# Transposing u by DMA on the SyncE queue in place of TensorE matmuls, in a retention-and-mixer kernel

## The chip, the cores and the metric

The kernel runs on one core of one Trainium2 chip. The metric is the time on the device in microseconds (us), the median of several runs. A core has five engines that run side by side and wait for each other by semaphores: TensorE (PE, matrix products into PSUM), VectorE (DVE), ScalarE (ACT), GpSimd (POOL) and SyncE (SP, which here only issues DMAs). DMAs move data by 16 DMA engines that all queues share. Each engine and each queue takes its instructions strictly in its own order: an instruction that waits holds up all behind it on that engine.

## The reference

Four batches of 768 tokens, 8 heads of 64, so a model width of 512. First a retention layer gives x, then a mixer:

```python
# retention, for each head h with decay gamma[h]
state = gamma * state + k[t] (outer) v[t]
y[t]  = scale * q[t] @ state
x     = y, heads side by side             # (4, 768, 512)
# mixer
h  = x^T @ U @ V                          # along the tokens, rank 32
u  = x + h^T
ch = relu(u @ w_ch1) @ w_ch2              # 512 -> 2048 -> 512
out = u + ch
```

## The kernel before

The retention is computed in chunks of 128 tokens, six chunks to a batch, in bf16 with sums in fp32. The program is software-pipelined over the batches. Batch 0's retention runs first (turn0, score0, mix0, L484 to L536), while the first weights are loaded. After that there are four stages. In stage b the MLP of batch b-1 is computed on PE in 64 groups of matmuls ("pieces", mlp_pieces), and woven in between them is the retention of batch b (turn_chunk, score4, mix4) and the low-rank part of the mixer. The last stage has the MLP of batch 3 alone.

One MLP runs in this order on PE: 16 groups "up" (L414) over tokens 0 to 511, each of four 128x512 matmuls, then 16 groups "up" over tokens 512 to 767, each of four 128x256 matmuls, then 24 groups "down" (L437) of four. ACT (L421) and DVE (L419) take the up results through the ReLU into gT, DVE adds u to the down results (L442), and POOL's queue stores them (L403).

The "up" matmuls need u with the model width on the partitions: uT[b], of 4 blocks of 128 by 768 tokens. u itself is made with the tokens on the partitions. Three functions make u and uT:

- lr_proj(b) (L366) projects x of the whole batch by U, so it needs all six chunks.
- lr_expand(b, j0, nj) (L375) multiplies by V for nj groups of 128 tokens, and DVE adds x and writes u (L382).
- lr_turn(b, j0) (L387) turns two groups of 128 tokens: eight matmuls against the identity (L391) into the PSUM tile R, and one copy by ACT into uT (L395, recorded as L75, the line of the helper evac).

For batch 0, tokens 0 to 511 are turned and summed in another way (x_turn, and L577 to L581); only its tokens 512 to 767 go by lr_turn. For batches 1 to 3, lr_turn is called three times: for tokens 0 to 255 and 256 to 511 towards the end of the stage in which the batch's retention is computed, and for 512 to 767 early in the stage in which its MLP runs.

The order on each engine is the order in which the program text issues it (manual_schedule). weave goes through the pieces of an MLP, and before each piece calls the marks whose place, a share of the MLP's nominal cost, has been reached. The places of lr_turn are these:

```python
LR = {1: (0.89, 0.92, 0.945, 0.97), 2: (0.71, 0.75, 0.83, 0.89)}   # proj, expand, turn, turn
marks = [(0.02, part(lr_expand, b - 1, 4, 2)), (0.06, part(lr_turn, b - 1, 4))]   # b > 1
marks = [(0.03, part(lr_expand, 0, 4, 2)), (0.10, part(lr_turn, 0, 4)), ...]      # b == 1
```

Loads of q, k, v and the weights are all issued by SP, in the order of the list feed. The function feed_more issues as many of them as there are free buffers, whenever a buffer is given up in program order (19 buffers in the pool rin; one buffer each for qin and kin, in which batches 1 to 3 hold all of q or k, loaded by load_whole, L115; the others are loaded at L142). POOL casts and scales the loaded chunks to bf16 (prep_turned, prep_natural, L86 and L88). A batch's kin and qin are loaded only once POOL has cast the last chunk of the batch before. In program order these loads are issued well ahead of the marks of lr_turn: when lr_turn(0, 4) is called, all loads of batch 1 have been put into SP's queue, and when the first lr_turn of batch b is called, all those of batch b+1.

The uT and u tiles have two buffers each, so that the batches take turns.

Of the kernel before, what the change touches and what calls it, by code (L numbers as in the profile page):

```python
# [16 lines left out]
def kernel(  # L17
# [11 lines left out]
    nc = tc.nc  # L29
    P = 128  # L30
# [6 lines left out]
    NCB = DM // P  # L37
# [22 lines left out]
    R = [psum.tile([P, 2, 512], fp32, tag="r0", name="r0")]  # L60
# [12 lines left out]
    def evac(eng, dst, src):  # L73
        if eng == "A":
            nc.scalar.activation(dst, src, AF.Copy)  # L75
        else:
            nc.vector.tensor_copy(out=dst, in_=src)
# [106 lines left out]
    for h in range(H):  # L184
        r = ds(32 * (h // 2), 32)
# [6 lines left out]
    ident = consts.tile([P, P], bf16)  # L192
# [4 lines left out]
    for i in range(NST):  # L197
        t = consts.tile([P, 4, P], bf16, name=f"state{i}")
# [157 lines left out]
    us, uTs, pcs = {}, {}, {}  # L356
# [27 lines left out]
                R[g][:, :, :nj * P].rearrange("p c (j e) -> p c j e", j=nj),  # L384
                v4(xs[b][:, ds(j0, nj), e]), op=ALU.add)

    def lr_turn(b, j0, eng="A"):  # L387
        r = R[j0 // 2 % 2]
        for c in range(NCB):
            for jj in range(2):  # L390
                nc.tensor.matmul(r[:, c // 2, ds(256 * (c % 2) + P * jj, P)],  # L391
                                 us[b][:, j0 + jj, ts(c, P)], ident, start=True,
                                 stop=True)
        evac(eng, uTs[b][:, :, ds(j0 * P, 2 * P)],
             r.rearrange("p n (c t) -> p (n c) t", c=2))  # L395


    stores = []

# [147 lines left out]
    with tc.tile_pool(name="psum0", bufs=1, space=bass.MemoryType.PSUM) as psum0:  # L547
# [21 lines left out]
        for j in range(NCK):  # L569
            for c in range(NCB):  # L570
                nc.tensor.matmul(p_p[ds(RK * c, RK), :P], Ub[:, j],
                                 xs[0][:, j, ts(c, P)], start=(j == 0),
                                 stop=(j == NCK - 1))
# [27 lines left out]
    for b in range(1, B):  # L601
        w = min(b, 2)
        if b > 1:
            marks = [(0.02, part(lr_expand, b - 1, 4, 2)),
                     (0.06, part(lr_turn, b - 1, 4))]
        else:
            marks = [(0.03, part(lr_expand, 0, 4, 2)), (0.10, part(lr_turn, 0, 4)),
                     (0.16, part(lr_expand, 0, 0, 4))]
        step = AT[w][1][0] - AT[w][0][0]
        for ci in range(NCK):  # L610
            s_at, m_at = AT[w][ci]
            marks.append((s_at - 0.6 * step, part(turn_chunk, b, ci)))
            marks.append((s_at, part(score4, b, ci)))
            marks.append((m_at, part(mix4, b, ci)))
            if ci + 3 < NCK:
                marks.append((s_at - 0.55 * step, part(prep_chunk, b, ci + 3)))
            elif b + 1 < B:
                marks.append((m_at + 0.05, part(prep_chunk, b + 1, ci - 3)))

        def mixed():  # L620
            lr_open(b)
            lr_proj(b)
        marks += zip(LR[w], (mixed, part(lr_expand, b, 0, 4), part(lr_turn, b, 0),
                             part(lr_turn, b, 2)))
        weave(mlp_pieces(b - 1), marks)
    b = B - 1
# [32 lines left out]
```

## Time and profile before

| | |
|---|---|
| median of 3 runs | 254.31 us (253.49 to 254.50) |
| the profiled execution | 254.5 us |
| its span, first to last instruction | 252.7 us |
| PE busy | 221.9 us (88%) |
| DVE, ACT, POOL busy | 102.6, 87.6, 100.0 us |
| granted TensorE clock, mean | 0.961 of full speed |
| data moved by DMA | 35.45 MB, 140 GB/s over the span |
| SyncE queue's data (q1) | 26.71 MB, 62800 packets |
| matmuls of lr_turn (L391) | 80 of 219 ns, pipelined |
| copies of lr_turn on ACT (uT<-r) | 10 of 1022 ns |

How to read the lines that follow: PE is the matmul part of TensorE, PEld its weight loads, SPq and POOLq the queues of SyncE and GpSimd. A row of 40 digits cuts the span into 40 equal slices, each digit the busy share in tenths; PEclk is the clock that the throttle granted to TensorE. In lists in order of time a line gives the start and the length in us, the engine, the line of the kernel, the operation, output<-input, and in brackets how long the engine was idle before and what ended this. In the chain of work that ended last, a line gives start, length and what the chain was made of. In the list of waits the numbers are the sum in us, the number of times and the longest one.

### The profile page before, as it was taken

The page shows a single profiled execution, that of the slowest core. Times are in us where ns is not written, and L with a number is a line of the kernel's source. Part 1 is how long each engine was busy: PE and PEld are TensorE (multiplying, and loading weights), DVE is VectorE, ACT ScalarE, POOL GpSimd, SP SyncE. Part 2 cuts the span into 40 slices and gives each one's busy share as a digit, 9 for nine tenths or more (in the row PEclk, how much of TensorE's full clock was granted, in tenths as well). Part 3 has the DMA queues.
Part 4 walks back from the last instruction along what each step waited for, and adds up shares of the span by engine and source line. Part 5 has one row for each costly group of instructions (what it writes and reads, how often), then busy time and mean ns, then how long its engine had stood idle before and what let it go on. Part 6 is the DMA issues. An engine that isn't in the chain of part 4 may idle for free.

```text
span 252.7 us, 5495 instructions
## 1 busy us (share of the span) xinstructions
PE 221.9 (88%) x2304; PEld 122.7 (49%) x2304; DVE 102.6 (41%) x193; ACT 87.6 (35%) x182; POOL 100.0 (40%) x138
## 2 busy tenths in 40 slices
PE   0784789954889998999999999999999999999991
PEld 0573534543545544445754454447644544584440
DVE  5433344413147434566544525556544242221121
ACT  3556335441323312555541033556410315450000
POOL 4776565057765207994108815720001010000110
PEclk9999779996599999999999999999999999999998
DMA  8999899999958999957999932000011120001211
GB/s 158 218 218 191 247 350 256 217 211 212 208 97 176 266 233 205 228 148 167 207 206 218 263 109 86 0 4 4 0 44 64 65 83 0 3 0 41 86 62 63
DMA packets 66857, 35.45 MB, mean 140 GB/s; under 512 B 51856, under 2 KB 63120, under 8 KB 66832
## 3 DMA queue, kind: packets, MB, share of 16 engines
q1 hardware_dynamic: 62800, 26.71, 52.1%
q0 software_dynamic: 4032, 8.39, 11.9%
q8 instruction: 18, 0.29, 0.5%
q14 instruction: 7, 0.06, 0.1%
HBM read 30.90 MB, written 6.29 MB: 147 GB/s over the span
## 4 chain that ended last, share of the span: by engine, by line
PE 45%; issue 20%; DMA 16%; SPq 10%; POOL 3%; DVE 2%; ACT 1%; POOLq 0%; DVEq 0%; ACTq 0%
PE mlp L437 21%; PE mlp L414 16%; SPq L142 9%; DMA in<-in_moe_w_ch_dram 5%; DMA qin<-in_q_dram 5%; DMA w2b<-in_moe_w_ch_dram 4%; PE r L347 2%; PE r L314 2%; POOL out_dram L403 2%; DMA Vf<-in_moe_V_dram 2%; SPq L115 1%; PE r L338 1%; DVE a L320 1%; PE r L391 1%; PE st L299 1%
## 5 line engine op out<-in xcount | busy, mean ns | idle before, releaser
L414 PE MATMUL mlp<-uT,w1b 128*128 128x512 bf16 (+1 forms) x512 | 92.3, 335 | 1.7 <-ACT uT L75 0.9
L437 PE MATMUL mlp<-w2b,gT 128*128 128x512 bf16 x384 | 89.5, 382 | 1.2 <-DMA w2b<-in_moe_w_ch_dram 1.2
L414 PEld LDWEIGHTS <-w1b 128*128 128x128 bf16 x512 | 49.4, 100 | 34.7 <-issue 3.7
L421 ACT ACTIVATE gT<-mlp 128x512 bf16<-128x512 f32 (+1 forms) x88 | 42.7, 490 | 53.6 <-PE mlp L414 52.7
L437 PEld LDWEIGHTS <-gT 128*128 128x128 bf16 x384 | 35.7, 98 | 40.7 <-issue 1.8
L403 POOL DMA_DIRECT2D out_dram<-o x24 | 13.3, 555 | 89.5 <-DVE o L442 89.5
L442 DVE TENSOR_TENSOR o<-mlp,u 128x512 f32<-128x512 f32 x24 | 16.6, 692 | 50.0 <-PE mlp L437 50.0
L419 DVE TENSOR_SCALAR gT<-mlp 128x512 bf16<-128x512 f32 (+1 forms) x40 | 22.0, 552 | 34.8 <-PE mlp L414 34.8
L320 DVE TENSOR_TENSOR a<-r,mask 128x512 bf16<-128x512 f32 x36 | 23.2, 685 | 18.8 <-PE r L314 17.1
L88 POOL TENSOR_TENSOR qi<-qin,gqT 128x512 bf16<-128x512 f32 x18 | 18.7, 1045 | 20.0 <-DMA qin<-in_q_dram 20.0
L75 ACT ACTIVATE x<-r 128x256 bf16<-128x256 f32 x36 | 11.8, 381 | 28.9 <-PE r L347 28.7
L88 POOL TENSOR_TENSOR vd<-in,gk 128x512 bf16<-128x512 f32 x18 | 18.7, 1043 | 7.8 <-DMA in<-in_v_dram 4.6
L75 ACT ACTIVATE uT<-r 128x1024 bf16<-128x1024 f32 x10 | 10.2, 1022 | 28.0 <-PE r L391 28.0
L86 POOL CAST ki<-kin 128x512 bf16<-128x512 f32 x18 | 13.5, 761 | 14.5 <-DMA kin<-in_k_dram 14.5
L382 DVE TENSOR_TENSOR u<-r,x 128x512 bf16<-128x512 f32 (+1 forms) x16 | 14.6, 952 | 6.6 <-PE r L375 6.6
L520 DVE TENSOR_TENSOR a<-r,mask 128x512 bf16<-128x512 f32 x12 | 7.7, 686 | 14.1 <-PE r L515 14.1
L314 PE MATMUL r<-qT,kT 32*128 32x128 bf16 x288 | 7.6, 225 | 5.8 <-DVE qT L264 5.8
L86 POOL CAST w1b<-in 128x512 bf16<-128x512 f32 x16 | 9.8, 613 | 5.5 <-DMA in<-in_moe_w_ch_dram 5.1
L314 PEld LDWEIGHTS <-kT 32*128 32x128 bf16 x288 | 4.5, 96 | 11.5 <-issue 10.3
L264 DVE STREAM_TRANSPOSE qT<-qi 128x256 f32<-128x256 f32 x18 | 7.3, 406 | 6.7 <-POOL qi L88 6.7
L489 PE MATMUL qk<-ident,qd 128*128 128x128 bf16 x24 | 3.5, 295 | 6.5 <-DVE ident L193 6.5
L75 ACT ACTIVATE qkT<-qk 128x1024 bf16<-128x1024 bf16 x6 | 6.1, 1024 | 8.7 <-PE qk L491 8.7
(70 smaller groups left out, 147.5 us busy)
## 6 DMA issues: line engine op xcount, KB each, us to landing
in<-in_v_dram SPq DMA_DIRECT2D x24, 256.0 KB, 5.7
out_dram<-o POOLq DMA_DIRECT2D x24, 256.0 KB, 2.6
in<-in_k_dram SPq DMA_DIRECT2D x18, 256.0 KB, 5.5
kin<-in_k_dram SPq DMA_DIRECT2D x12, 384.0 KB, 7.8
qin<-in_q_dram SPq DMA_DIRECT2D x12, 384.0 KB, 13.0
in<-in_moe_w_ch_dram SPq DMA_DIRECT2D x16, 256.0 KB, 6.2
w2b<-in_moe_w_ch_dram POOLq DMA_DIRECT2D x4, 512.0 KB, 9.9
in<-in_q_dram SPq DMA_DIRECT2D x6, 256.0 KB, 5.2
```

The lines of the kernel that those rows point to most:

```text
L75: nc.scalar.activation(dst, src, AF.Copy)
L86: e.tensor_copy(out=dst, in_=src)
L88: e.tensor_tensor(dst, src, scale, op=ALU.mult)
L142: nc.sync.dma_start(out=t, in_=src)
L314: nc.tensor.matmul(R[hp // 2][:, hp % 2, ts(i, P)], turned("kT", b, ci, i, c, r), turned("qT", b, ci, i, c, r), start=(c == 0), stop=(c == 1))
L320: nc.vector.tensor_tensor(a[:, ds(4 * g, 4)].rearrange("p (n i) m -> p n i m", n=2), R[g][:, :, :256].rearrange("p n (i m) -> p n i m", i= ...
L403: nc.gpsimd.dma_start(out=dst, in_=src)
L414: nc.tensor.matmul(g_p[:, :sz], w1b[:, c, ts(m, P)], uTs[b][:, c, ds(lo, sz)], start=(c == 0), stop=(c == NCB - 1))
L419: nc.vector.tensor_relu(gT[:, m, ds(lo, sz)], g_p[:, :sz])
L421: nc.scalar.activation(gT[:, m, ds(lo, sz)], g_p[:, :sz], AF.Relu)
L437: nc.tensor.matmul(ch, gT[:, m, ts(j, P)], w2b[:, m], start=(m == 0), stop=(m == NM - 1))
L442: nc.vector.tensor_tensor(o_sb, ch, us[b][:, j], op=ALU.add)
```

## The change

lr_turn no longer uses PE, PSUM and ACT. For each of its two groups of 128 tokens it issues a transposing DMA on SP, from u (128 tokens by 512, bf16) to the four 128x128 blocks of uT. Nothing else is changed: its callers and the places of the marks stay, and batch 0's tokens 0 to 511 are turned on PE as before.

```diff
-    def lr_turn(b, j0, eng="A"):
-        r = R[j0 // 2 % 2]
-        for c in range(NCB):
-            for jj in range(2):
-                nc.tensor.matmul(r[:, c // 2, ds(256 * (c % 2) + P * jj, P)],
-                                 us[b][:, j0 + jj, ts(c, P)], ident, start=True,
-                                 stop=True)
-        evac(eng, uTs[b][:, :, ds(j0 * P, 2 * P)],
-             r.rearrange("p n (c t) -> p (n c) t", c=2))
-
+    def lr_turn(b, j0):
+        for j in (j0, j0 + 1):
+            nc.sync.dma_start(out=uTs[b][:, :, ts(j, P)], in_=us[b][:, j],
+                              transpose=True)
```

It is called ten times, so there are 20 such DMAs: two for batch 0, six for each of the others. In SP's order the two of batch 0 stand after the last load of v of batch 1 and before the load of kin of batch 2; those of batch 1 after the last load of batch 2 and before kin of batch 3; those of batches 2 and 3 after the last load of all.

## The prediction

> **What bounds the kernel now.** I first read the engine shares: PE is busy 88% of the span, no other engine over 41%. Next the 40 slices (6.3 us each), which tell where PE is not alone:
>
> ```profile
> PE   0784789954889998999999999999999999999991
> PEclk9999779996599999999999999999999999999998
> DMA  8999899999958999957999932000011120001211
> ```
>
> The span has two halves. Up to about 148 us the DMA engines are as full as PE, first ahead of it, then beside it; after that PE works alone. Then the list of waits of the SyncE queue (SP), and its instructions in order of time (start, length, line, count):
>
> ```profile
> 35.91 3.65 SPq L115 DMA_DIRECT2D kin<-in_k_dram  x4
> 40.02 7.23 SPq L115 DMA_DIRECT2D qin<-in_q_dram  x4
> 47.35 19.86 SPq L142 DMA_DIRECT2D in<-in_v_dram  x6
> 75.99 2.11 SPq L115 DMA_DIRECT2D kin<-in_k_dram  x4
> ...
> 105.79 0.89 SPq L142 DMA_DIRECT2D in<-in_v_dram  x1
> 114.31 1.87 SPq L115 DMA_DIRECT2D kin<-in_k_dram  x4
> ```
>
> SP issues in program order, and is busy with loads of the next batch without a hole from 35.9 to 67.2 us, again from 76.0 to 106.7 and from 114.3 to 144.3. The holes end on POOL:
>
> ```profile
> SPq L115 <- POOL ki L86: 16.2, 2, 8.7
> ```
>
> That is, the next batch's kin (one buffer) may be loaded only when POOL has cast the last chunk of the present one. Last, the timeline of PE, and the chain, around one transposition:
>
> ```profile
> 36.05 1.29 DVE L382 TENSOR_TENSOR u<-r,x 128x512 bf16<-128x512 f32 x2 [2.83 <-PE r L375]
> 39.17 1.02 ACT L75 ACTIVATE uT<-r 128x1024 bf16<-128x1024 f32 x1
> 104.79 0.45 PE r L391 x8
> 148.45 0.45 PE r L391 x8
> ```
>
> Eight matmuls of L391 put 0.45 us on the chain; the copy by ACT lies beside other work.
>
> **What is removed.** lr_turn is called ten times: 80 matmuls, 80 weight loads, ten copies on ACT. PE saves 10 x 0.45 = 4.5 us at most. The 10.2 us of ACT copies count nothing: ACT is 35% busy and PE waited for uT in all for 0.9 us. PSUM room is freed too, worth nothing: R's next writers come later.
>
> **What is added.** Twenty transposing DMAs, each of one 128x512 bf16 tile (128 KB), put into SP's program order where the marks stand. The order of all engines otherwise stays. Three things matter: what stands before them in SP, how long they take, and who waits.
>
> Who stands before them: the pair of batch 0 (tokens 512 to 767) comes after the last in_v load of batch 1, the one that SP finishes issuing at 67.2. The first four of batch 1 come after the last in_v of batch 2 (ends 106.7), those of batch 2 after the last in_v of batch 3 (ends 144.3). Nothing stands before those of batch 3. And they use the same queue of data as the loads: with the DMA engines full, a transposition moves only when the loads ahead have moved. By windows of time the DMA share falls at 72 to 73 (1.07 to 0.30), at 110.3 and at 148.2.
>
> How long they take: no row shows one. Low end: an in_v load is 256 KB in runs of 256 bytes and SP sends one each 1.14 us when the engines are full (its issues between 10.9 and 19); half as many bytes, 0.57 us. High end: the median landing of an in_v load, 5.7 us, each one alone. Nearest is the load, with the same runs, but turning is work on top; I take 1.5 us each, and 1.5 us until the last has landed (a 256 KB store lands in 2.6 us, of which 1.1 is moving). Two take 4.5 us, four 7.5; at the ends 2.6 and 3.8, or 12.9 and 24.3.
>
> The Trainium skill states two prices. "VectorE: DVE Perf Modes", section The three transpose paths, gives 1309 ns for a 128x128 block by DMA against 390 ns on TensorE and advises TensorE where PSUM will do: it speaks against this change, and four blocks in a row would be 5.2 us, an estimate from that page by which the sum would end at some 345 us. "Advanced Engine Details and Errata", section X-Bar Transpose (TRN2), says transposing DMAs are as fast as plain ones: the low end. No row here decides between them; for TensorE the trace has 0.056 us a block (0.45 / 8), far below the page's price.
>
> **First stall.** PE's 256-wide matmuls of batch 0 need those two transpositions. They begin at 48.9 (the last five 512-wide ones start at 47.8, 0.216 each), 0.45 earlier without L391: 48.4. The data queue is free at 73.0, plus 4.5: PE goes on at R = 77.5. What is late next: everything behind that matmul on PE, the ReLUs of ACT and DVE, and behind DVE's the transposes of chunk 0 (L264).
> From that point to lr_expand of batch 1 PE took 48.9 to 96.0 = 47.1 us before. Of it 5.84 + 0.81 + 1.24 were waits for qT, kT and w2b, which will all be there by 77.5; and the clock was half for 8.3 us of busy time:
>
> ```profile
> 54.00:60.00 6.00, 0.25 (x5) 0.92 1.28 206
> 60.00:61.00 1.00, 0.91 (x18) 0.50 1.23 205
> 69.00:70.00 1.00, 1.00 (x20) 0.84 1.22 196
> ```
>
> (window, its length, PE busy, granted clock, DMA share, GB/s.) Half of 8.3 is 4.15 lost. So 47.1 - 7.89 - 4.15 = 35.1 us of work remain. An idle PE comes back at half clock: at 60 this cost 4.15, at 32.5 about 1.5; I add 3. lr_expand then is at 77.5 + 35.1 + 3 = 115.6, and after three more groups (2.6) and its own 0.4 PE wants uT of batch 1 at 118.6.
>
> **Second stall.** Loads of batch 2 wait for POOL's last cast of batch 1, and this for PE: 14 groups of four 256-wide matmuls (14 x 0.43, half of the 512-wide ones), natural_k and scores (0.56), mask (1.29), mix and state (0.57), then vd and ki on POOL (1.80): R + 10.3, with the clock 13.3, so kin goes out at 90.8 in place of 76.0, 14.8 later. The loads are bound by the DMA engines and take as long as before: free at 110.3 + 14.8 = 125.1; four transpositions: 132.6. PE waits 14 us, and batch 1's first matmul, before at 101.7, is 30.9 later. The clock again: 2.5.
>
> **Third and fourth.** Batch 2's: loads done at 148.2 before, plus 7.5 = 155.7; PE would be there at 153.05 less three L391 groups (1.35) = 151.7. A stall of 4.0, net +2.65, and 1 for the clock. Batch 3's: u is ready at 196.4, plus 7.5 = 203.9; PE is there at 204.97 - 1.35 = 203.6: net -1.05. The pairs for tokens 512 to 767 of batches 1 to 3 have some 14 us of matmuls as cover and an idle SP: nothing, and -0.45 at the last.
>
> **Sum**, against the profiled execution (254.5, span 252.7; the median of three is 254.31): 30.9 + 2.5 + 2.65 + 1 - 1.05 - 0.45 = +35.55; 254.5 + 35.5 = **290 us**. At the low price (3.8 and 2.6 us): R = 75.6, clock 2, loads 11.9 later, free at 122.2, plus 3.8 = 126.0, +24.3, clock 2, a stall of 0.3 at batch 2, and -1.35 - 1.35 - 0.45: 278. At the high price: R = 85.9, +56.1, then +19.5, +15.8 and 7 for the clock, -0.45: 352.
>
> **Rivals.**
> - One stall only: batch 2's loads catch up behind the first stall, so that PE meets no second. Then PE goes from 118.6 on, +16.9, less 3.15: 268. For it: at 32 to 40 us the DMA engines moved 361 GB/s, against 230 from 76 to 110. Against it: those were the long runs of w1; in_k and in_v never went so fast, and kin waits for POOL.
> - Slow transpositions, 3 us or more each. R = 80.5, +39.9 at batch 1, +2.5, +8.65 and 2.5 at batch 2, +4.95 and 2 at batch 3, -0.45: 315. For it: nothing excludes it. Against it: the equal runs of the loads.
> - Hidden, faster: SP reaches the transpositions when u is ready (37.4 us) and they overtake loads. Then all ten groups are saved: 254.5 - 4.5 = 250. It decides where the first pair lands before 48.4. Against it: 27 more us of loads issued in order before them.
>
> **Chances.** Two or more stalls at up to 2.5 us each 0.70; slow 0.15; one stall 0.10; hidden 0.03; something between that ends equal 0.02. The time is that of the first. The range goes from the one-stall case's upper edge, 270, to 320, just past the 3 us price. 0.5% (1.3 us) is about what a measurement can tell from no change: faster 0.03, same 0.02, slower 0.95.
>
> **What would show it.** In the profile after: SP's transpositions begin at about 67, not 37; PE idle from 48.4 to 77 or so, released by the DMA into uT; kin of batch 2 some 15 us later; a second wait for uT of 10 to 17 us at about 118; clock 0.5 after each; no wait of over 5 us after batch 2. If the pair lands before 60, or if PE's second wait is missing, the argument on the queue is wrong; if the waits are there but twice as long, the price is.

## The result, and the profile after

The changed kernel takes 277.02 us (median of 4 runs, 275.99 to 278.54) against 254.38 us before (253.49 to 254.5): a ratio of 1.090, with a 95% interval of 1.084 to 1.097. It is slower by 22.6 us. The forecast was 290 in a range of 270 to 320. The profiled execution took 276.31 us, its span is 274.5 us.

First the 40 slices of the page of the changed kernel (6.9 us each), in the same rows as before:

```profile
PE   0776699100099999907999999999999999999992
...
PEclk9997689955559999966999999999999999999998
DMA  8999999999900999991199998420000253000111
```

PE has two holes that it did not have: the digits 1 0 0 0 (48 to 75 us) and later 0 7 (117 to 130). In and after each the granted clock is low (5 5 5 5, then 6 6). DMA is full up to the end of each hole and almost empty after it (0 0, then 1 1): the loads that should follow have not been released.

Next SP's instructions in order of time:

```profile
45.88 20.92 SPq L142 DMA_DIRECT2D in<-in_v_dram  x6
66.91 6.87 SPq L389 DMA_TRANSPOSE uT<-u  x2
87.57 1.88 SPq L115 DMA_DIRECT2D kin<-in_k_dram  x4
...
116.24 1.62 SPq L142 DMA_DIRECT2D in<-in_v_dram  x1
117.97 13.46 SPq L389 DMA_TRANSPOSE uT<-u  x6
136.32 1.86 SPq L115 DMA_DIRECT2D kin<-in_k_dram  x4
...
164.62 1.37 SPq L142 DMA_DIRECT2D in<-in_v_dram  x1
169.63 62.70 SPq L389 DMA_TRANSPOSE uT<-u  x12
```

Batch 0's pair is issued at 66.9, 29 us after its u was ready (at 38.2); kin of batch 2 at 87.6 in place of 76.0; batch 1's first four at 118.0. And PE's matmuls of the same stretches (in brackets the idle time before, and what ended it):

```profile
75.50 7.67 PE L408 MATMUL mlp<-uT,w1b 128*128 128x256 bf16 x44 [26.08 <-DMA uT<-u]
...
125.37 1.86 PE L408 MATMUL mlp<-uT,w1b 128*128 128x512 bf16 x4 [9.04 <-DMA uT<-u]
...
177.22 1.03 PE L408 MATMUL mlp<-uT,w1b 128*128 128x512 bf16 x4
```

Two waits, 26.1 and 9.0 us, both ended by the landing of uT. The third line, the first matmul of batch 2's MLP, has no wait. The sums over the whole span, from the list of waits, say the same from the other side:

```profile
PE mlp L408 <- DMA uT<-u: 35.1, 2, 26.1
...
POOL ki L86 <- DVE kT L264: 16.5, 2, 9.0
```

The second line is how PE's holes reach the loads, one wait behind each hole. The longer one, in order of time on DVE and POOL:

```profile
77.40 0.42 DVE L413 TENSOR_SCALAR gT<-mlp 128x256 bf16<-128x256 f32 x1 [28.12 <-PE mlp L408]
...
80.30 0.44 DVE L264 STREAM_TRANSPOSE kT<-ki 128x256 f32<-128x256 f32 x1
...
80.80 0.76 POOL L86 CAST ki<-kin 128x512 bf16<-128x512 f32 x1 [9.00 <-DVE kT L264]
...
86.78 0.77 POOL L86 CAST ki<-kin 128x512 bf16<-128x512 f32 x1
```

POOL's casts of batch 1 wait for DVE's block transposes (L264), which stand behind ReLUs (L413) that have no input while PE is stopped. The last cast ends at 87.5, and kin of batch 2 goes out at 87.57.

A table of the first matmul of each MLP shows where the 21.8 us of span went (us from the start of the span, from the timelines of the two kernels):

| | batch 1 | batch 2 | batch 3 | end |
|---|---|---|---|---|
| before | 101.71 | 153.05 | 204.97 | 252.7 |
| after | 125.37 | 177.22 | 227.22 | 274.5 |
| stage longer by | +23.66 | +0.51 | -1.92 | -0.45 |

### The profile page after: what moved, and what is told of

Read it like the earlier page. It is cut to its first block, busy times and chain, and to the rows that moved or that the text cites. A ratio compares the mean times of both kernels' runs of the same rounds, so it can differ in the third digit from the quotient of the medians.

```text
span 274.5 us, 5345 instructions
## 1 busy us (share of the span) xinstructions
PE 218.4 (80%) x2224; PEld 117.9 (43%) x2224; DVE 102.6 (37%) x193; ACT 78.0 (28%) x172; POOL 100.7 (37%) x138
## 4 chain that ended last, share of the span: by engine, by line
PE 28%; issue 28%; SPq 21%; DMA 17%; POOL 4%; POOLq 0%
PE mlp L408 16%; SPq L142 16%; PE mlp L431 8%; DMA in<-in_v_dram 7%; DMA in<-in_moe_w_ch_dram 4%; DMA kin<-in_k_dram 4%; SPq L389 4%; POOL out_dram L397 2%; DMA uT<-u 2%; SPq L115 2%; PE r L314 1%; PE r L347 1%; POOL vd L88 1%; POOL ki L86 1%; PE st L299 1%
## 5 line engine op out<-in xcount | busy, mean ns | idle before, releaser
L408 PE MATMUL mlp<-uT,w1b 128*128 128x512 bf16 (+1 forms) x512 | 94.0, 341 | 35.9 <-DMA uT<-u 35.1
L431 PE MATMUL mlp<-w2b,gT 128*128 128x512 bf16 x384 | 87.7, 380 | 0.0
L408 PEld LDWEIGHTS <-w1b 128*128 128x128 bf16 x512 | 50.1, 102 | 71.3 <-DMA uT<-u 26.5
L397 POOL DMA_DIRECT2D out_dram<-o x24 | 13.3, 556 | 93.4 <-DVE o L436 93.4
L413 DVE TENSOR_SCALAR gT<-mlp 128x512 bf16<-128x512 f32 (+1 forms) x40 | 22.2, 554 | 63.3 <-PE mlp L408 63.2
L320 DVE TENSOR_TENSOR a<-r,mask 128x512 bf16<-128x512 f32 x36 | 23.2, 685 | 14.7 <-PE r L314 12.8
L88 POOL TENSOR_TENSOR vd<-in,gk 128x512 bf16<-128x512 f32 x18 | 18.7, 1044 | 16.2 <-issue 5.6
L88 POOL TENSOR_TENSOR qd<-in,gq 128x512 bf16<-128x512 f32 x6 | 6.3, 1042 | 5.6 <-DMA in<-in_q_dram 5.6
L86 POOL CAST kd<-in 128x512 bf16<-128x512 f32 x12 | 7.3, 611 | 2.3 <-issue 1.4
L264 DVE STREAM_TRANSPOSE kT<-ki 128x256 f32<-128x256 f32 x18 | 7.9, 436 | 0.0
```

The lines of the kernel that those rows point to most:

```text
L86: e.tensor_copy(out=dst, in_=src)
L88: e.tensor_tensor(dst, src, scale, op=ALU.mult)
L320: nc.vector.tensor_tensor(a[:, ds(4 * g, 4)].rearrange("p (n i) m -> p n i m", n=2), R[g][:, :, :256].rearrange("p n (i m) -> p n i m", i= ...
L397: nc.gpsimd.dma_start(out=dst, in_=src)
L408: nc.tensor.matmul(g_p[:, :sz], w1b[:, c, ts(m, P)], uTs[b][:, c, ds(lo, sz)], start=(c == 0), stop=(c == NCB - 1))
L413: nc.vector.tensor_relu(gT[:, m, ds(lo, sz)], g_p[:, :sz])
```

## The experiments

Each undoes one part of the change, or moves transpositions or loads to another place.

**Only batch 0's pair back on TensorE.** Under the condition stand the eight matmuls and the ACT copy of the kernel before; else the DMAs.

```diff
-    def lr_turn(b, j0):
+    def lr_turn(b, j0, eng="A"):
+        if b == 0:
+            r = R[j0 // 2 % 2]
...
+            return
         for j in (j0, j0 + 1):
             nc.sync.dma_start(out=uTs[b][:, :, ts(j, P)], in_=us[b][:, j],
                               transpose=True)
```

> Only batch 0's pair goes back to TensorE; the other 18 transpositions stay on SyncE. Theory (place in the queue, two stalls one behind the other): the first stall of 26 us is gone, loads of batch 2 run from 76 to 107 us again, batch 1's four transpositions come behind them and land 7.4 us later (117.9 to 125.2 in the changed kernel), at 114, where PE before had uT at 101.7. So +12.4, +1.9 for the clock, less 1.35, 1.9 and 0.45 for groups of L391 saved: 265 us, with one wait of PE for uT of 13 to 15 us. Rival (the transposing DMAs are slow beside loads, wherever they stand): the first stall was only its first sign, the same 7.4 us would be paid at each batch, and about 258 to 260 would be left. Rival (the two stalls hide each other): 277 as in the changed kernel.

Measured 264.94 us (ratio 1.043, 1.039 to 1.048), where 265 was expected. From its timeline, SP and PE:

```profile
106.68 13.55 SPq L399 DMA_TRANSPOSE uT<-u  x6
...
114.19 1.86 PE L418 MATMUL mlp<-uT,w1b 128*128 128x512 bf16 x4 [16.74 <-DMA uT<-u]
```

The first wait is gone, and the four transpositions go out as the loads of batch 2 end, at 106.7, where the trace of before has the end of those loads. They land 7.5 us later, at 114.2. So the second wait was there all along; in the changed kernel the first one hides a part of it: there PE comes to batch 1's MLP 18.9 us later than here (116.3 against 97.4), and uT only 11.2 us later (125.4 against 114.2).

**Only batch 1's first four back on TensorE** (condition `b == 1 and j0 < 4`), run twice.

> Only batch 1's first four groups of tokens go back to TensorE; batch 0's pair stays on SyncE. Theory: the first stall is as in the changed kernel (PE goes on at 75.5), lr_expand of batch 1 ends at 113.6, and with its 5.2 us of TensorE transpositions, ACT copies and matmuls uT is there at 118.8 in place of 101.7: +17.1, less 1.35, 1.9 and 0.45: 268 us, one wait of 26 us. The two stalls are then not a sum (13 + 11 would be over the 22.6 seen): the second overlaps with the lateness of the first. Rival (two independent costs that add up): 277 less what the run with batch 0 on TensorE shows.

> The kernel with only batch 1's first four on TensorE once more, since its runs lay apart (265 to 271). Theory: 268 with one wait of 26 to 29 us; a spread that stays comes from the length of that one wait, that is from when the loads of batch 1 have moved.

Measured 270.25 us (one run of 265.21, the other three from 270.01 to 270.79), and in the second series 269.09 us (268.88 to 269.47; ratio 1.059, 1.055 to 1.063); 268 was expected. Why one run was 5 us shorter was not seen; what follows goes by the second series. From the second one's timeline of PE:

```profile
77.11 6.74 PE L418 MATMUL mlp<-uT,w1b 128*128 128x256 bf16 x44 [28.46 <-DMA uT<-u]
...
119.70 1.02 PE L418 MATMUL mlp<-uT,w1b 128*128 128x512 bf16 x4 [0.25 <-ACT uT L75]
```

One wait of 28.5 us and no second one. The two costs are not a sum: batch 0's part alone costs 15.0 us (5.9% of 254.6), batch 1's alone 11.0 (4.3% of 253.9), together 26, and the changed kernel lost 22.6, although the gain from the seven other calls is counted twice in the 26. With that gain taken out of each, at the 3.7 us of the expectations' sum (1.35 + 1.9 + 0.45), the losses alone are 18.7 and 14.7 against 26.3 for both: by this estimate 7 us of the second wait lie under the lateness of the first. The waits themselves say 7.7 (16.74 alone, 9.04 behind the first).

**Both back on TensorE** (`b == 0 or (b == 1 and j0 < 4)`): seven of the ten calls stay on SP. Run twice.

> Batch 0's pair and batch 1's first four go back to TensorE; the seven other calls (14 transpositions) stay on SyncE. Theory: these have landed long before PE wants them, so no wait for uT is left and their TensorE groups are saved: 1.35 + 1.9 + 0.45 less 0.5 for a ReLU's wait that may return: 251.0 us, faster than before by 1.2 to 1.5%. Rival (transposing DMAs disturb the loads beside them or are too slow): 254.5 or more.

> The kernel with batch 0's pair and batch 1's first four on TensorE once more. Its MLP stages from batch 1 on were 2.8 us shorter than before in the trace, but batch 1's first matmul came 1.1 later than before (PE waited 3.4 us for w2b in place of 1.2), in code that is the same. Theory: this is scatter of the load-bound first 100 us, so the median is 251 to 253. Rival (a systematic loss in the first stage): batch 1's first matmul is late again by 1 us or more.

Measured 253.19 us (ratio 0.994, 0.991 to 0.998) and 252.74 us (0.993, 0.989 to 0.996). It is faster than before, by 0.7% and not by the 1.3% expected. In the first trace there was no wait for uT and batch 1's first matmul was at 102.83; in the second it was at 100.17, before that of the old kernel (101.71). The lateness of the load-bound first part is thus scatter, and not a loss of the change. But the second trace has a wait at batch 2 (and one of 0.26 us at batch 3):

```profile
153.64 1.77 PE L418 MATMUL mlp<-uT,w1b 128*128 128x512 bf16 x4 [2.77 <-DMA uT<-u]
```

**The pair ahead of the loads.** All 20 transpositions on SP, but lr_expand and lr_turn of batch 0's last two groups are made before the MLP begins, and batch 1's loads are held until then.

```diff
-        n_cast[0] = 2 * NCK
...
     R.append(psum1.tile([P, 2, 512], fp32, tag="r1", name="r1"))
+    lr_expand(0, 4, 2)
+    lr_turn(0, 4)
+    n_cast[0] = 2 * NCK
+    feed_more()
...
-            marks = [(0.03, part(lr_expand, 0, 4, 2)), (0.10, part(lr_turn, 0, 4)),
-                     (0.16, part(lr_expand, 0, 0, 4))]
+            marks = [(0.16, part(lr_expand, 0, 0, 4))]
```

> All 20 transpositions stay on SyncE, but batch 0's lr_expand and pair are made before the first group of its MLP, and the loads of batch 1 are put into SyncE's queue behind that pair. Theory (place in the queue): the pair issues at about 36 to 39, lands before 45, the first stall is gone though the transposition is the same; batch 1's loads are 3 us later; the second stall stays: 265 + 3 = 268 us, as the run with batch 0's pair on TensorE and a little more. Rival (slow in itself beside loads): PE still waits for batch 0's pair beyond 49, and the time stays at 275 or more.

Measured 269.83 us (1.061, 1.057 to 1.066). Its timeline of SP and PE:

```profile
37.24 2.62 SPq L389 DMA_TRANSPOSE uT<-u  x2
39.91 2.10 SPq L115 DMA_DIRECT2D kin<-in_k_dram  x4
...
118.24 1.86 PE L408 MATMUL mlp<-uT,w1b 128*128 128x512 bf16 x4 [17.38 <-DMA uT<-u]
```

The same pair, on the same queue, costs PE no wait when it stands ahead of kin. Loads and all that follows them are 4 us later (kin of batch 2 at 80.85 against 76.60 in the first experiment), a little more than the 3 expected. The second wait stays as it was.

**Batch 1's four ahead of the last loads.** On top of the first experiment, the loads of chunks 3 to 5 of batch 2 are held until lr_turn(1, 2) has been called.

```diff
+            if key[0] in "kv" and key[1] == 2 and key[2] >= 3 and not turned_1:
+                return
...
+        if (b, j0) == (1, 2):
+            turned_1.append(True)
+            feed_more()
```

> Batch 0's pair on TensorE as in the run before that did this, and the loads of batch 2's chunks 3 to 5 (six in_k and in_v) are put into SyncE's queue behind batch 1's four transpositions in place of before them. Theory: these issue when u is ready, at 98.8, and take 7.4 us to land as in the changed kernel: 106.2 in place of 114, PE waits 7 us in place of 15: 254.5 + 4.5 + 1.5 - 3.7 = 257 us. The delayed loads cost nothing, they are wanted 20 us later. Rival (the wait comes from the load on the DMA engines, not from the order in the queue): 263 to 265, as without the gate.

Measured 257.36 us (1.014, 1.009 to 1.019), as expected.

```profile
98.98 5.80 SPq L402 DMA_TRANSPOSE uT<-u  x4
...
106.18 1.87 PE L424 MATMUL mlp<-uT,w1b 128*128 128x512 bf16 x4 [6.92 <-DMA uT<-u]
```

They go out when u is ready and land at 106.2. A wait of 6.9 us stays: when the first of them goes out, PE has only 0.3 us of matmuls left (it stops at 99.26), and the four take 7.2 from the first issue until PE goes on. So here the length of the transpositions costs the time, and no longer their place.

**Another queue.** All transpositions issued by ScalarE (`nc.scalar.dma_start`), at the same marks.

> All 20 transpositions as in the changed kernel, but issued by ScalarE in place of SyncE, at the same marks. Theory (place in SyncE's queue): they no longer stand behind the loads; batch 0's pair issues when u is ready, at 37 to 40, lands before 48: no first stall. Batch 1's four issue from 98.8 to 104 and land at 107 to 109, beside the loads of batch 2: PE waits some 7 us in place of 9 after a first stall. ScalarE is held up by the wait and by issuing (1.3 us each), which may cost PE 1 us at each batch. Sum 254.5 + 6 + 1.9 + 1 to 3 - 3.7: 259 to 262 us. Rival (what counts is the total order of data on the DMA engines, whichever queue): both stalls stay, 275 or more.

Measured 270.86 us (1.065, 1.061 to 1.069). Both theories missed. From the timelines of ACT's queue, SP and PE, and the waits of SP:

```profile
39.02 3.78 ACTq L389 DMA_TRANSPOSE uT<-u  x2
...
51.41 1.85 SPq L115 DMA_DIRECT2D qin<-in_q_dram  x4
...
51.98 5.16 PE L408 MATMUL mlp<-uT,w1b 128*128 128x256 bf16 x44 [2.28 <-DMA uT<-u]
...
111.98 1.86 PE L408 MATMUL mlp<-uT,w1b 128*128 128x512 bf16 x4 [8.70 <-DMA uT<-u]
```

```profile
SPq L142 <- DMA uT<-u: 35.7, 10, 14.1
...
SPq L115 <- DMA uT<-u: 11.2, 1, 11.2
```

As expected, the pair goes out at 39.0 and the long first wait becomes 2.3 us. But the pair lands 12.4 us after its issue, beside the loads of kin, and the loads of SP now wait for transpositions, 46.9 us in all: qin, which goes out at 40.0 in the kernel before and at 39.4 in the changed one, does so at 51.4, when the pair has landed. In the listing of the program every DMA of SP and ACT waits for the one eight places before it, because eight completion semaphores go round; a slow transposition on one queue thus stops the loads on the other. Of the 15.7 us by which this span is longer than before, 10.3 are there at batch 1's first matmul (111.98 against 101.71), and 3.6 more come in the stage of batch 2's MLP, which was not followed further. Why the pair needed 12.4 us was not settled either.

**A gate for batch 2 too.** The kernel with seven calls on SP, and the last four loads of batch 3 held until lr_turn(2, 2), in the same way as above.

```diff
+            if key[0] in "kv" and key[1] == 3 and key[2] >= 4 and not turned_2:
+                return
```

> The kernel with batch 0's pair and batch 1's first four on TensorE, and besides the last four loads of batch 3 (chunks 4 and 5) put into SyncE's queue behind batch 2's four transpositions. Theory: what kept that kernel at 252.7 to 253.2 in place of 251 is a short wait for batch 2's uT in a part of its executions (2.8 us in one trace, none in the other), when the loads before it move late; with fewer loads ahead it is gone: 251 to 252 us. Rival (the rest is lost elsewhere, in the load-bound first 100 us): 252.7 to 253.2 as without the gate.

Measured 251.53 us (ratio 0.9875, 0.984 to 0.991): faster than the kernel before by 1.25%, as expected. Its list of waits has none for a uT that comes by DMA. From its timeline of SP:

```profile
144.55 5.15 SPq L402 DMA_TRANSPOSE uT<-u  x4
```

Without the gate these four went out at 145.8 and 146.1 in the two traces. The gate's own share, some 0.5%, is likely but not shown: the interval without it reaches from 0.989 to 0.996 in the second series, and overlaps with this one.

**Batch 2's four on TensorE instead** (`b == 0 or (b < 3 and j0 < 4)`), five calls left on SP.

> TensorE turns batch 0's pair and the first four of batches 1 and 2; five calls stay on SyncE, all with an idle queue or long cover. Theory: no wait for uT in any execution, five groups saved: 254.4 - 5 x 0.45 = 252.1 us. Rival (the transpositions beside batch 3's loads cost nothing): slower by 0.9 us than the kernel that keeps them on SyncE.

Measured 253.22 us (0.995, 0.992 to 0.998), 1.1 more than the theory's sum, though its list of waits has none for a uT that comes by DMA. In the same series the kernel with the gate is 1.7 us faster by the medians, but it differs in two things, two more calls on SP and the gate. The kernel with seven calls and no gate differs in the two calls alone, and its ratios (0.994 and 0.993) have intervals that overlap with this one's. So batch 2's two calls on SP are not shown to gain anything without the gate; with it, calls and gate together do.

## Why the prediction was right

**Direction and mechanism.** Right up to batch 1's MLP. SP reached batch 0's pair at 66.9 (67.2 was said), PE was idle for 26 us from 49.4 to 75.5 (48.4 to 77.5 was said), kin of batch 2 came late (11.6 us; 14.8 was said), a second wait followed at batch 1 and a low clock after each. The second wait was 9.0 us, a little under the 10 to 17 that were given as its sign; the stalls forecast for batches 2 and 3 did not come. The experiments show the reason, place in the queue: the same pair costs PE no wait when it stands ahead of the loads, holding six loads back takes the second wait from 16.7 to 6.9 us, and undoing each part removes its own wait and no other.

**Size.** The sum was +35.5, the profiled execution shows +21.8; 277.0 lies in the lower part of the range, 13 us under the forecast. By the table, batch 1's first matmul is 23.66 us later where 30.9 was said, the stage after it 0.51 longer where 2.5 + 2.65 + 1 = 6.15 was said, the next 1.92 shorter for 1.05, and the last 0.45 shorter as said. These terms were too large:

- The price behind a full queue. I let the loads drain first (3.6 us after the last issue at 106.7) and then put 7.5 us for four transpositions after it, 11.1 together. Issue and draining overlap: in the changed kernel the four are issued from 117.97 on and have landed at 125.24, 7.4 us after the last load was issued; in the experiments 7.5 (106.68 to 114.19) and 7.2. This is 3.7 of the error. From the chain of the changed kernel, the issues and the landings of the two waits:

```profile
66.91 5.22 SPq L389
...
72.58 2.78 DMA uT<-u
...
117.97 1.71 SPq L389
...
122.74 2.50 DMA uT<-u
```

- The first landing: R, the time at which PE goes on, was 75.5, not 77.5, for the same reason: the first of the pair was being issued from 66.9 to 72.1, while the loads drained. 2.0.
- The clock. From the windows of the changed kernel (stretch, its length, PE busy and its matmuls, granted clock, DMA share, GB/s):

```profile
76.00:77.00 1.00, 1.00 (x7) 0.50 0.00 0
80.00:81.00 1.00, 1.00 (x7) 0.50 0.07 16
81.00:82.00 1.00, 1.00 (x10) 0.96 0.00 0
...
128.00:129.00 1.00, 1.00 (x4) 0.57 0.00 0
129.00:130.00 1.00, 1.00 (x6) 1.00 0.00 0
```

  Half clock from 75.5 to 81.0 loses 2.8 us, where 3 was taken; from 125.4 to 129 about 1.8, where 2.5 was taken. The release of kin came 12.1 us after R and not 13.3, which is 1.2 more of batch 1's lateness.
- Stalls at batches 2 and 3: 4.0 and 0.3 us, and 1 for the clock, were forecast, none came. With the loads shifted together with the matmuls, batch 2's four went out at 169.63 on an almost empty queue and were there before PE came at 177.22. The step that was too large is again draining plus transposition added end to end: the last load of batch 3 ended its issue at 144.3 in the kernel before, and with the 7.4 measured uT would be there at 151.7, just when PE was said to come.

**The gains.** 4.5 us at most from the matmuls was right in kind: the last two stages are 1.92 and 0.45 us shorter. Of the 1.92, 1.35 are the three groups; another 0.52 is a wait of PE for a ReLU at 154.8 in the kernel before that the changed one does not have, and why it went was not tested. In the stage of batch 1's MLP the 1.35 saved are eaten by the clock after the second wait (1.8).

**The price of one transposition** was bounded from 0.57 to 5.7 us and set at 1.5. On an idle queue SP issues one each 1.27 us and it lands 2.4 us after its issue; so the chosen value was near. The sum at the low price, 278, ends 1 us from the time measured, but by luck: it takes 0.57 us for each.

The Trainium skill's "Advanced Engine Details and Errata", section X-Bar Transpose (TRN2), makes a transposing DMA as fast as a plain one. At the pace of SP's queue the runs do not bear this out: 1.27 us a tile, against 0.57, the estimate from half a plain load. By the time that the packets took on the DMA engines the two are closer. In the run on ScalarE's queue, the 20 transpositions took 6.0% of the 268.4 us, 0.81 us each, and SP's loads took 49.7% for 26.71 MB, 0.65 us for as many bytes. Nor does the 1309 ns of "VectorE: DVE Perf Modes", section The three transpose paths, hold for each of the four blocks in turn: all four have landed in 2.4 us. That page's advice (section Rules for kernel authors), TensorE where PSUM will do, fits the three calls with no cover; the seven others together gain 0.7% on SP.

**The rivals.** One stall only: its 268 us is near what each half of the change gives by itself (265 and 269), but its mechanism did not occur. Batch 2's loads did not catch up behind the first stall: from the first kin to the last issue they took 30.3 us (87.57 to 117.86) against 30.7 before (75.99 to 106.68). Slow transpositions: no, 1.27 us each. Hidden: no transposition overtook loads on SP, but seven of the ten calls are hidden by the cover that they have, with a wait of 2.8 us at batch 2 in one trace, and with none where the last loads were held back (251.5 us).

## What to carry to other kernels

A DMA that takes over work from a busy engine can cost far more by its place in the queue than by its length: list what stands ahead of it in that queue at the moment its input is ready, let the draining and its own issue overlap (added end to end they were too much here), and compare with the work left until its result is used. Where little work is left, as at batch 1, its length remains as a wait (6.9 us), whatever its place. Do this call by call: here three of ten calls turned a gain of 0.7% into a loss of 9%. Another issuing queue is no way out by itself: on ScalarE's the loads waited for the transpositions. A wait early in a pipelined kernel also delays what releases the next loads, so removing the first wait alone shows the second; try both before judging. Where the order matters, holding back a few loads that are needed late can win most of it: six held loads took the time from 264.9 to 257.4 us.

## What the runs showed of the hardware that was not expected

- A transposing DMA of 128x512 bf16 between places in SBUF occupied its issuing queue for 1.19 us at the least and 1.27 in the median, and landed in 2.4 us when nothing was ahead; behind loads the issue took up to 5.2 us in the changed kernel and 6.7 us with batch 1's four on TensorE, and on ScalarE's queue, beside loads, the landing up to 12.4 us.
- The 20 transpositions count 10880 packets and 2.62 MB where they have a queue of their own (ScalarE's): 544 packets each, about as many as the tile has runs of 256 bytes (512).
- After 26 us of idleness TensorE ran at half clock for 5.5 us of full work, after 9 us for some 3.6 us; after the 2.8 us wait in the kernel with seven calls on SP its first four matmuls also took 1.77 us in place of 1.02.
